# Step 0's scores and exponentials move into the planned projections, and the plan's order changes

## The chip, the cores and the metric

The kernel runs on one core of a Trainium2 chip. The metric is the device time of one execution in microseconds; the time before is the median of three runs, 881.73 us (881.26 to 881.87). The profile is of one execution of its own, which took 882.3 us; its span from the first to the last instruction is 880.5 us, and the 1.8 us between lie outside the instructions.

## The reference

Two mixers read the same input x (2048 x 448, 16 heads of 28) and their outputs are blended by a gate. A looks at 8 positions with a stride of 2, B at all positions. The softmax of B is the bulk of the work.

```python
# A: W, dil = 8, 2
logits = jnp.einsum("bhsd,bhswd->bhsw", q, kg) * scale
logits = jnp.where(mask[None, None, :, :], logits, -1e9)
o = jnp.einsum("bhsw,bhswd->bhsd", _softmax(logits, axis=-1), vg)
# B
scores = jnp.einsum("bhqd,bhkd->bhqk", q, k) * (Dh ** -0.5)
o = jnp.einsum("bhqk,bhkd->bhqd", _softmax(scores, axis=-1), v)
...
g = _sigmoid((x * gate_w).sum(-1, keepdims=True))
return g * a + (1 - g) * b
```

## The kernel before

Everything is scheduled by hand: the order in which the program records instructions is the order in which each engine takes them. Each float32 operand of a product is split into a high and a low part, so a projection and a score are three products each (high x high, low x high, high x low).

**Projections.** 92 output tiles (`tiles`): 28 tiles of B's q and k (128 x 512), 16 of B's v and 48 of A's q, k and v (128 x 448). The first eleven (`FULL`) use the whole array. The next 80, tiles 11 to 90, come from a plan: `quarters()` deals each tile's 42 products to four quarters of 32 rows of the array, which run at the same time, and gives each tile one of the eight PSUM banks `PS[0]` to `PS[7]` (named r0 to r7). A tile's products that belong to different quarters come one quarter after the other. When a tile's last product is sent, ScalarE copies the bank (`qk_tile` or `copy_tile`; an A tile goes to a staging tile `ast` whose store is issued by SP's queue in `a_tile`).

**Maxima.** The softmax of B needs a maximum of a row of scores before the exponentials. Only the high parts are used for that: a maximum is one product of 30 rows in one quarter (`s1_mm`, line 152) and one VectorE reduction over 512 columns (`s1_quarter`, line 174, in the plan; `s1_max`, line 158, in the main loop). There are 1024 in 16 units of 64; 320 are sent in the plan (`MAXIMA`), 80 a quarter. The planner keeps clocks for PE's quarters, VectorE and ScalarE and the time at which each bank comes free. It sends a maximum when VectorE's queue, by its own clocks, is shorter than `HUNGER` (0.1 us) and a bank is free, and no quarter is more than one maximum ahead of another beyond `AHEAD`. q's high part for the next unit is loaded by `load_qhi` (line 104, into `QP`) when a unit is begun or done.

**Main loop.** 256 steps: unit u (four heads, 512 queries) and kt (128 keys). A step takes twelve products of scores (four heads by three, line 1212, `scores`), up to three maxima, two exponentials of two heads each by ScalarE (128 x 1024, line 1217) into pairs `P`, five of which rotate, and the four products with V of the step before (`do_av`, line 1178) into the bank `av`. PSUM is laid out anew for it: three tiles of two banks (T0, T1 and T2, which `ring` turns), the single bank `T1` (line 734) and `av`. A new tile of PSUM may be written only when every reader of the old ones in its banks has finished; `T1` and `av` come from one pool. VectorE's small work, GpSimd's work for mixer A and the loads are hung on the steps (`at`, `issue`, `item`). The last 20 steps are sent by `tail_steps` in an order of their own, with single exponentials of 128 x 512 (line 1355) among them, and the output projection ends the kernel.

**Between the two.** Step 0 is sent after the plan. As it has no step before it whose product with V could stand between its scores and those of step 1, the last projection tile (`last_tile`, line 603, eleven products of the whole array into `av`) stands there.

Of the kernel before, what the change touches and what calls it, by code (L numbers as in the profile page):

```python
# [26 lines left out]
def gated_mix_kernel(ctx: ExitStack, tc: tile.TileContext, xT, xn, gw, wA, wB, woAB, out):  # L27
# [129 lines left out]
    def s1_max(n, k, bank):  # L157
# [5 lines left out]
            finished.append(n // 64)  # L163
        s1c[0] = n + k


    count = [0] * 4

# [64 lines left out]
    if True:  # L233
# [192 lines left out]
        def quarters(n0, n1, maxima):  # L426
            todo = [[n for k in range(n0, n1, 5) for n in (k + i for i in TURN[q]) if n < n1] for q in range(4)]
            cols = {n: 512 if tiles[n][1] == "qk" else D for n in range(n0, n1)}
            left = {n: sum(len(quarter_order(n, q)) for q in range(4)) for n in cols}
            free, ready, sent, stay, home = [0.0] * 8, {}, [0] * 4, [[] for _ in range(4)], {}  # L430
            free[(n0 - 1) % 4] = 2.0
            end, begun = [0.0] * 4, [-1.0] * 4
            now_ = dve = act = issue = 0.0
            plan, round_ = [], []
            while any(todo) or any(stay):
                b = min(range(8), key=lambda i: free[i])

                def start(q, wait):
                    return max(max(issue, wait, begun[q]) + LOAD, end[q], now_)

                best = None
                for q in range(4):
                    wait = 0.0
                    if not stay[q]:
                        n = todo[q][0] if todo[q] else None
                        wait = ready.get(n, free[b]) if n is not None else 1e9
                    p = start(q, wait), 1, q, wait
                    m = start(q, free[b]), 0, q, free[b]
                    if sent[q] < min(maxima // 4, min(sent) + AHEAD + 1) and free[b] < 1e8:
                        lag = dve - m[0] - REACH  # L450
                        if (lag < HUNGER and free[b] <= max(issue, end[q] - LOAD) + 0.02) or (
                                p[0] < 1e8 and p[0] > m[0] + 0.18 and lag < HUNGER + 1.2):
                            p = m
                    if p[0] < 1e8 and (best is None or p < best):
                        best = p
                t, product_, q, wait = best
                if round_ and max(act, round_[0][0]) <= t:
                    act = max(act, round_[0][0]) + 0.64
                    plan.append((t, "round", round_.pop(0)[1]))
                issue, now_, begun[q] = max(issue, wait) + 0.003, t, t  # L460
                if not product_:
                    sent[q] += 1
                    end[q] = t + 0.2315
                    dve = max(dve, t + REACH) + SUM
                    free[b] = dve + 0.092 + WORD
                    plan.append((t, "max", q, b))
                    continue
                if not stay[q]:
                    n = todo[q].pop(0)
                    stay[q] = [(n, p) for p in quarter_order(n, q)]  # L470
                    first = n not in home
                    if first:
                        home[n] = b
                        free[b] = 1e9
                    ready[n] = 1e9
                else:
                    first = False
                n, p = stay[q].pop(0)
                end[q] = t + (0.2315 if cols[n] == 512 else 0.2045)
                left[n] -= 1  # L480
                last, leaves = not left[n], not stay[q]
                plan.append((t, "product", n, p, q, home[n], first, last, leaves and not last))
                if leaves:
                    ready[n] = t + REACH + NOP
                if last:
                    act = max(act, t + REACH)
                    free[home[n]] = act + (0.68 if cols[n] == 512 else 0.62) + WORD
                    act += 0.607 if cols[n] == 512 else 0.553
                    if cols[n] == 512:
                        round_.append((act + 0.1, n))  # L490
            return plan + [(now_, "round", n) for _, n in round_]


# [111 lines left out]
            a_tile(len(tiles) - 1, bank, i, j)  # L605


        FULL, MAXIMA = 11, 320

        parts = []  # L610

# [83 lines left out]
            behind(n)  # L695
        n = FULL
        before(n)
        plan = quarters(FULL, len(tiles) - 1, MAXIMA)
        turns.extend(x[0] + REACH for x in plan if x[1] == "product" and x[8])
        for t, kind, *x in plan:  # L700
            run_jobs(t)
            if kind == "max":
                s1_quarter(x[0], PS[x[1]])
                continue
            if kind == "round":
                qk_round(x[0])
                continue
# [481 lines left out]
    def scores(u, kt, cur):  # L1189
# [9 lines left out]
        for tok in WITH if k else ALONE:  # L1199
            if tok[0] == "s":  # L1200
                i = int(tok[1])
                if i < k:
                    s1_mm(n + i, bank[tok])
                if i == 0:
                    s1_max(n, 1, T1)
                elif i == 2 and k > 1:
                    s1_max(n + 1, k - 1, other[:, 0:k - 1, :])
                continue
            a, t = tok[0], int(tok[1])
            h = (int(a) + n) % 4  # L1210
            r = slice(32 * h, 32 * h + ROWS)
            nc.tensor.matmul(bank[a], (KH[g % 3], KH[g % 3], KL[g % 2])[t][r, ks], (qh, ql, qh)[t][r, :], start=(t == 0), stop=(t == 2))  # L1212
            if t == 2 and a in "20":
                if len(exps) < 5:
                    probs.append(pair("P"))
                p = probs[len(exps) % 5]
                e = nc.scalar.activation(p, one if a == "2" else mine, AF.Exp, scale=SCALE).ins  # L1217
                for o in exps[-5:-4]:
                    tc.declare_no_dep(e, o, query=mybir.DependencyQuery.ANY_SYNC,
                                      reason="PE has read what it wrote, and this one waits for PE")  # L1220
# [66 lines left out]
    def bank_of(m, b):  # L1287
        return m.tiles[b[0]][:, b[1], :] if b[0] else T1

    lastp = {}  # L1290

    def tail_steps(sts, m, waiting, begin, middle, finish):

        left = {}
# [4 lines left out]
        for tok in PERIOD:  # L1299
# [49 lines left out]
            else:  # L1349
# [4 lines left out]
                parts = [(id(p), c)]  # L1354
                e = nc.scalar.activation(p[:, c, :], bank, AF.Exp, scale=SCALE).ins
                m.read[banks[0]] = [*m.read.get(banks[0], ()), e][-3:]
            for part in parts:
                for o in lastp.get(part, ()):
                    tc.declare_no_dep(e, o, query=mybir.DependencyQuery.ANY_SYNC,
                                      reason="PE has read what it wrote, and this one waits for PE")  # L1360
                lastp[part] = [*lastp.get(part, ()), e][-3:]
# [8 lines left out]
    turn = [0]  # L1370

    def pair_p():
        p = probs[turn[0] % 5]
        turn[0] += 1
        return p

    def step_begin(u, kt, st):
        now[0] = st
# [20 lines left out]
    for u in range(NU):  # L1399
        g, b = divmod(u, NB)  # L1400
        for kt in range(NJ):
# [30 lines left out]

    assert s1c[0] == s1e and not finished
    m = Banks()
    turn[0] = len(exps) % 5
    for i, e in enumerate(exps[-5:]):
        p = probs[(len(exps) - 5 + i) % 5 if len(exps) >= 5 else i]
        lastp[id(p), 0], lastp[id(p), 1] = [e], [e]
    waiting = [(NJ * NU - TAIL - 1, prev, 0.5)]

    def tail_finish(st):
# [49 lines left out]
```

## Time and profile before

| | before |
|---|---|
| median of three runs | 881.73 us |
| profiled execution | 882.3 us, span 880.5 us |
| PE / VectorE / ScalarE / GpSimd busy | 99% / 85% / 69% / 62% of the span |
| granted TensorE clock | 1.000 |
| first to last product of the plan's quarters | 34.7 to 236.6 us |
| last tile's first matmul | 238.3 us |
| step 1's first score | 240.8 us |
| first of the 20 last steps | about 768 us |

A row of the timeline gives the start in us, the length, the engine, the line and the operation with its tiles, and how many instructions are merged in it; in brackets the idle time of the engine ahead of it and what ended it. Records of PE overlap, since its matmuls are pipelined and four quarters run at once. A row of a group gives count, busy time, mean length of one in ns, and the idle time ahead. A row of windows gives the stretch, the busy time and, behind x, how many instructions touch it.

### The profile page before, as it was taken

What the parts mean: (1) busy time and instruction counts of PE and PEld (TensorE: products, weight loads), DVE (VectorE), ACT (ScalarE), POOL (GpSimd) and SP (SyncE); (2) the same over time, 40 slices, a digit from 0 to 9 for tenths busy, and PEclk for the clock granted to TensorE, in tenths of its full rate; (3) what the DMA queues carried; (4) which work ended last, traced back from release to release, by engine and by line L of the source; (5) the groups of instructions that cost most, each with busy time, mean ns of one, the idle gap of its engine ahead of it and who ended that gap; (6) DMA issues with size and microseconds to landing.
All of it is one profiled execution on the core that took longest, in us unless ns stands there. A gap on an engine that the chain in (4) does not pass through costs nothing.

```text
span 880.5 us, 24214 instructions
## 1 busy us (share of the span) xinstructions
PE 874.7 (99%) x9988; PEld 522.6 (59%) x9988; DVE 747.7 (85%) x1128; ACT 609.2 (69%) x800; POOL 548.9 (62%) x439
## 2 busy tenths in 40 slices
PE   9999999999999999999999999999999999999998
PEld 6899999999844444444444344444444444434997
DVE  7699999999889999999999999999999999832220
ACT  6353323212388899898888988989989898898120
POOL 1157402110089789998899989999999799701000
PEclk9999999999999999999999999999999999999999
DMA  8858605545564232224235242442131222337781
GB/s 262 266 184 257 201 14 146 121 112 134 116 224 133 74 90 55 89 56 136 73 73 153 63 122 58 109 122 67 47 74 30 83 45 50 105 93 203 197 268 53
DMA packets 114199, 104.76 MB, mean 119 GB/s; under 512 B 75256, under 2 KB 82424, under 8 KB 113304
## 3 DMA queue, kind: packets, MB, share of 16 engines
q1 hardware_dynamic: 113656, 102.42, 41.2%
q8 instruction: 78, 1.28, 0.6%
q10 hardware_dynamic: 432, 0.79, 0.3%
q14 instruction: 33, 0.27, 0.1%
HBM read 62.20 MB, written 40.96 MB: 117 GB/s over the span
## 4 chain that ended last, share of the span: by engine, by line
PE 97%; DVE 1%; ACT 1%; DMA 0%; issue 0%; ACTq 0%
PE T L1212 29%; PE av L1178 29%; PE r L390 14%; PE r L385 8%; PE T L1046 8%; PE T L152 4%; PE r L152 3%; PE T L1329 2%; DVE MX L174 1%; DMA raw<-in_wB 0%; ACT P L1217 0%; PE av L603 0%; ACT ast L526 0%; ACT onhi L1103 0%; ACT wh L576 0%
## 5 line engine op out<-in xcount | busy, mean ns | idle before, releaser
L1217 ACT ACTIVATE P<-T 128x1024 f32<-128x1024 f32 x472 | 458.2, 1024 | 57.5 <-PE T L1212 55.8
L158 DVE TENSOR_REDUCE MX<-T 128x1 f32<-128x512 f32 x470 | 442.2, 953 | 32.2 <-PE T L152 17.9
L1178 PE MATMUL av<-P,V 128*32 128x512 f32 x2048 | 272.7, 605 | 0.0
L152 PE MATMUL T<-KH,QP 30*128 30x512 f32 x704 | 220.9, 458 | 0.0
L1212 PEld LDWEIGHTS T<-QH,KH 30*128 30x128 f32 x944 | 86.8, 181 | 212.6 <-ACT P L1217 196.5
L1212 PE MATMUL T<-QH,KH 30*128 30x512 f32 x944 | 199.9, 488 | 0.5 <-ACT ast L526 0.3
L174 DVE TENSOR_REDUCE MX<-r 128x1 f32<-128x512 f32 x320 | 197.8, 683 | 1.6 <-PE r L152 0.8
L1212 PE MATMUL T<-QH,KL 30*128 30x512 f32 x944 | 176.0, 394 | 0.0
L1212 PE MATMUL T<-QL,KH 30*128 30x512 f32 x944 | 173.7, 389 | 0.0
L390 PE MATMUL r<-wh,xh 32*128 32x448 f32 (+1 forms) x1008 | 152.1, 366 | 0.0
L390 PE MATMUL r<-wl,xh 32*128 32x448 f32 (+1 forms) x882 | 146.8, 362 | 0.0
L390 PE MATMUL r<-wh,xl 32*128 32x448 f32 (+1 forms) x756 | 140.2, 362 | 0.0
L813 POOL TENSOR_TENSOR prod<-qt,kt 128x896 f32<-128x896 f32 x64 | 135.4, 2116 | 3.9 <-DMA kt<-a_scr 3.9
L390 PEld LDWEIGHTS r<-wh,xh 32*128 32x128 f32 x1008 | 130.1, 184 | 1.4 <-ACT zt L538 0.5
L152 PE MATMUL r<-KH,QP 30*128 30x512 f32 x320 | 123.4, 400 | 0.0
L390 PEld LDWEIGHTS r<-wl,xh 32*128 32x128 f32 x882 | 121.2, 184 | 0.1
L390 PEld LDWEIGHTS r<-wh,xl 32*128 32x128 f32 x756 | 111.2, 184 | 0.1
L874 POOL TENSOR_TENSOR oat<-oat,prod 128x896 f32<-128x896 f32 x48 | 101.4, 2112 | 2.0
L152 PEld LDWEIGHTS T<-KH,QP 30*128 30x128 f32 x704 | 86.0, 181 | 25.9 <-ACT P L1217 14.9
L869 POOL TENSOR_TENSOR prod<-vt,L 128x896 f32<-128x896 f32 x56 | 95.5, 1705 | 0.3
L1212 PEld LDWEIGHTS T<-QL,KH 30*128 30x128 f32 x944 | 88.7, 184 | 0.0
L1212 PEld LDWEIGHTS T<-QH,KL 30*128 30x128 f32 x944 | 87.3, 182 | 0.1
(144 smaller groups left out, 1170.4 us busy)
## 6 DMA issues: line engine op xcount, KB each, us to landing
a_scr<-ast SPq DMA_DIRECT2D x24, 448.0 KB
qk_hi<-qkh SPq DMA_DIRECT2D x22, 256.0 KB
rbc<-rs SPq DMA_DIRECT2D x64, 64.0 KB
QP<-qk_hi SPq DMA_DIRECT2D x64, 56.0 KB
KL<-qk_lo SPq DMA_DIRECT2D x16, 224.0 KB
QH<-qk_hi SPq DMA_DIRECT2D x64, 56.0 KB
QL<-qk_lo SPq DMA_DIRECT2D x64, 56.0 KB
qt<-a_scr SPq DMA_DIRECT2D x8, 448.0 KB
```

Of the source, the lines that this page charges most:

```text
L152: nc.tensor.matmul(bank, qhis[u][h % 2][r, 128 * qs:128 * qs + 128], KH[u // NB % 3][r, 512 * kc:512 * kc + 512], start=True, stop=True)
L158: i = nc.vector.tensor_reduce(MX[:, n % NMX:n % NMX + k], bank, axis=X, op=ALU.max)
L174: nc.vector.tensor_reduce(MX[:, n % NMX:n % NMX + 1], bank, axis=X, op=ALU.max)
L385: i = nc.tensor.matmul(bank, ws[c][rows, k, t[4]:t[4] + 128], x, start=first, stop=last)
L390: i = nc.tensor.matmul(bank[:, 0:cols], x, ws[c][rows, k, 0:cols], start=first, stop=last)
L813: nc.gpsimd.tensor_tensor(out=p, in0=qt[c], in1=kvt["k", c % 2][:, HALO - DIL * w:HALO - DIL * w + NJ, :], op=ALU.mult)
L869: nc.gpsimd.tensor_tensor(out=dst.rearrange("p j (h d) -> p j h d", d=DH), in0=kvt["v", c % 2][:, HALO - DIL * w:HALO - DIL * w + NJ, :].r ...
L874: nc.gpsimd.tensor_tensor(out=ows[c % 2][:, :, 0:56] if w == W - 1 else oat[c], in0=oat[c], in1=oat[c, w], op=ALU.add)
L1046: writes(bank, nc.tensor.matmul(bank[:, cols], src, wo[c][k][:, cols], start=(first and k == ks[0] and i == 0), stop=(last and k == ks[-1] ...
L1178: nc.tensor.matmul(av[32 * h:32 * h + 32, :], V[:, kt, 4 * g + h, :], tiles_[h], start=(kt == 0), stop=(kt == NJ - 1), skip_group_check=True)
L1212: nc.tensor.matmul(bank[a], (KH[g % 3], KH[g % 3], KL[g % 2])[t][r, ks], (qh, ql, qh)[t][r, :], start=(t == 0), stop=(t == 2))
L1217: e = nc.scalar.activation(p, one if a == "2" else mine, AF.Exp, scale=SCALE).ins
```

## The change

Four things change.

1. Each quarter of the plan gets one item more at its end: the three score products of one head of step 0 (`score`). Its bank is the one that comes free first among seven; when a head's third product is sent, ScalarE takes the exponential of that one bank (128 x 512) into half a pair `P`. The main loop's step 0 then sends neither scores nor maxima, takes `first` as its exponentials, and goes on to `last_tile`.
2. The bank that is left first (other than the one of the tile before the plan) trades its number with bank 7, which `av` occupies, and `av` has a pool of its own, so that the last tile waits for that bank alone.
3. `MAXIMA` is 324 in place of 320, and `HUNGER` is a table of 26 values, one for each 8 us of the plan, in place of one value.
4. What tells the scheduler that a wait is implied already (`probability`), and the turn of the five pairs (`pair_p`), are written once for all three places that take exponentials.

```diff
+    def score(t, h, bank):
+        qh, ql = Qs[0]
+        r = slice(32 * h, 32 * h + ROWS)
+        nc.tensor.matmul(bank, (KH[0], KH[0], KL[0])[t][r, 0:128], (qh, ql, qh)[t][r, :], start=(t == 0), stop=(t == 2))
+        if t == 2:
+            if not len(first) % 2:
+                pair_p()
+            p, c = probs[len(first) // 2], len(first) % 2
+            first[h] = p[:, c, :]
+            probability([(id(p), c)], nc.scalar.activation(first[h], bank, AF.Exp, scale=SCALE).ins)
...
-        HUNGER, AHEAD = 0.1, 1
+        AHEAD, STRETCH = 1, 8.0
...
-            todo = [[n for k in range(n0, n1, 5) for n in (k + i for i in TURN[q]) if n < n1] for q in range(4)]
+            todo = [[n for k in range(n0, n1, 5) for n in (k + i for i in TURN[q]) if n < n1] + [n1 + q] for q in range(4)]
...
+                s = min(range(7), key=lambda i: free[i])
...
-                        if (lag < HUNGER and free[b] <= max(issue, end[q] - LOAD) + 0.02) or (
-                                p[0] < 1e8 and p[0] > m[0] + 0.18 and lag < HUNGER + 1.2):
+                        h = hunger[min(int(m[0] / STRETCH), len(hunger) - 1)]
+                        if (lag < h and free[b] <= max(issue, end[q] - LOAD) + 0.02) or (
+                                p[0] < 1e8 and p[0] > m[0] + 0.18 and lag < h + 1.2):
...
+                if n >= n1:
+                    plan.append((t, "score", p, q, home[n]))
+                    if last:
+                        act = max(act, t + REACH) + 0.494
+                        free[home[n]] = act + 0.1 + WORD
+                    continue
...
+            b = min((i for i in range(8) if i != (n0 - 1) % 4), key=lambda i: free[i])
+            swap = {b: 7, 7: b}
...
-        FULL, MAXIMA = 11, 320
+        FULL, MAXIMA = 11, 324
...
+        HUNGER = (0.26, 0.3, 0.14, 0.1, 0.1, 0.26, 0.1, 0.03, 0.26, 0, 0, 0.1, 0.18, 0.26, 0.1, 0.1, 0.1, 0.26, 0.26, 0.18, 0.03, 0.3, 0.35, 0.18, 0.1, 0.26)
...
     T1 = pool.tile([128, 512], F32, name="T1")
+    pool = ctx.enter_context(tc.tile_pool(name="psw", bufs=1, space=bass.MemoryType.PSUM))
     av = pool.tile([128, 512], F32, name="av")
...
-            for a in scores(u, kt, cur):
-                if a == 2:
-                    run("mid", st)
+            if st:
+                for a in scores(u, kt, cur):
+                    if a == 2:
+                        run("mid", st)
+            else:
+                cur, left = first, 0
+                run("mid", st)
```

**PE around the last tile.** These are PE's rows of before from the plan's last product (line 390) to the last tile (line 603); r0 to r7 are the plan's banks, T0 to T2 and T1 those of the main loop, QH and QL0 the high and low part of q, KH0 and KL0 those of k, and line 152 is a maximum.

```order
L390 MATMUL r2_136<-wh6_3643,xl1_208 128x448 x3
L1212 MATMUL T2_5199<-QH_4396,KH0_167 128x512 x2
L152 MATMUL T1_5203<-KH1_168,QP10_175 128x512
L1212 MATMUL T2_5199<-QL0_171,KH0_167 128x512 x2
L1212 MATMUL T1_5195<-QH_4396,KH0_167 128x512 x2
L1212 MATMUL T2_5199<-QH_4396,KL0_169 128x512 x2
L1212 MATMUL T1_5195<-QL0_171,KH0_167 128x512 x2
L152 MATMUL T0_5191<-KH1_168,QP11_176 128x512
L152 MATMUL T0_5191<-KH1_168,QP10_175 128x512
L1212 MATMUL T1_5195<-QH_4396,KL0_169 128x512 x2
L603 MATMUL av_5204<-wh6_3643,xh3_206 128x448 x4
```

After the change PE's last rows ahead of the last tile (now line 648) are these; line 187 is a score product of step 0, line 418 a product of the plan.

```order
L187 MATMUL r0_128<-QL0_171,KH0_167 128x512
L187 MATMUL r3_140<-QH_4399,KH0_167 128x512
L418 MATMUL r1_132<-wh6_3644,xl1_208 128x448
L187 MATMUL r0_128<-QH_4399,KL0_169 128x512
L187 MATMUL r3_140<-QL0_171,KH0_167 128x512
L418 MATMUL r1_132<-wh6_3644,xl1_208 128x448
L187 MATMUL r3_140<-QH_4399,KL0_169 128x512
L187 MATMUL r2_136<-QH_4399,KH0_167 128x512
L152 MATMUL r5_148<-KH1_168,QP10_175 128x512
L187 MATMUL r2_136<-QL0_171,KH0_167 128x512
L187 MATMUL r2_136<-QH_4399,KL0_169 128x512
L648 MATMUL av_5238<-wh6_3644,xh3_206 128x448 x4
```

The scores of step 0 moved from the main loop's banks into the plan's, the plan's last products stand among them, and the last tile follows the last score product. The last product into r7, whose bank `av` takes, stands 18 matmuls ahead of the last tile.

**ScalarE at the same place.** Its rows of before, from the copies of the plan's last tiles on (P are the exponentials, nmt and nmv the negated maxima of a unit):

```order
L526 ACTIVATE ast_5169<-r6_152 128x8x56
L526 ACTIVATE ast_5172<-r5_148 128x8x56
L526 ACTIVATE ast_5172<-r2_136 128x8x56
L1217 ACTIVATE P_5219<-T2_5199 128x1024
L1217 ACTIVATE P_5228<-T1_5195 128x1024
L195 ACTIVATE nmt_5232<-m_5230 128x16
L196 ACTIVATE nmv_5233<-m_5230 128x16
L526 ACTIVATE ast_5169<-av_5204 128x8x56
```

And after the change (line 193 is an exponential of one head, 571 a copy, 223 and 224 the negated maxima):

```order
L193 ACTIVATE P_5171<-r2_136 128x512
L571 ACTIVATE ast_5177<-r7_156 128x8x56
L571 ACTIVATE ast_5190<-r4_144 128x8x56
L193 ACTIVATE P_5171<-r0_128 128x512
L571 ACTIVATE ast_5177<-r1_132 128x8x56
L193 ACTIVATE P_5203<-r3_140 128x512
L193 ACTIVATE P_5203<-r2_136 128x512
L223 ACTIVATE nmt_5241<-m_5239 128x16
L224 ACTIVATE nmv_5242<-m_5239 128x16
L571 ACTIVATE ast_5190<-av_5238 128x8x56
```

Two exponentials of 1024 columns became four of 512, and they stand among the copies; the copy of r7 has one exponential right ahead of it. On SP's queue the four loads of q for unit 6 (`QP`), which stood behind the last but one staging tile's store, now stand ahead of it.

More of the change, by code (lines that the diff above doesn't have):

```diff
@@ L164, in s1_max, with pair_p, probability @@
         s1c[0] = n + k
+    turn = [0]
+    lastp = {}
+    first = {}
+    def pair_p():
+        if len(probs) < 5:
+            probs.append(pair("P"))
+        turn[0] += 1
+        return probs[(turn[0] - 1) % 5]
+    def probability(parts, e):
+        for part in parts:
+            for o in lastp.get(part, ()):
+                tc.declare_no_dep(e, o, query=mybir.DependencyQuery.ANY_SYNC,
+                                  reason="PE has read what it wrote, and this one waits for PE")
+            lastp[part] = [*lastp.get(part, ()), e][-3:]
+    def score(t, h, bank):
[8 more added lines that the diff above has]
+            probability([(id(p), c)], nc.scalar.activation(first[h], bank, AF.Exp, scale=SCALE).ins)
     count = [0] * 4
@@ L445, in quarters @@
                         n = todo[q][0] if todo[q] else None
-                        wait = ready.get(n, free[b]) if n is not None else 1e9
+                        wait = 1e9 if n is None else free[s] if n >= n1 else ready.get(n, free[b])
                     p = start(q, wait), 1, q, wait
@@ L490, in quarters @@
                         round_.append((act + 0.1, n))
+            if sum(sent) < maxima:
+                return None
+            b = min((i for i in range(8) if i != (n0 - 1) % 4), key=lambda i: free[i])
+            swap = {b: 7, 7: b}
+            where = {"max": 3, "score": 4, "product": 5}
+            plan = [(*x[:where[x[1]]], swap.get(x[where[x[1]]], x[where[x[1]]]), *x[where[x[1]] + 1:])
+                    if x[1] in where else x for x in plan]
             return plan + [(now_, "round", n) for _, n in round_]
@@ L1213, in scores @@
             if t == 2 and a in "20":
-                if len(exps) < 5:
-                    probs.append(pair("P"))
-                p = probs[len(exps) % 5]
+                p = pair_p()
                 e = nc.scalar.activation(p, one if a == "2" else mine, AF.Exp, scale=SCALE).ins
-                for o in exps[-5:-4]:
-                    tc.declare_no_dep(e, o, query=mybir.DependencyQuery.ANY_SYNC,
-                                      reason="PE has read what it wrote, and this one waits for PE")
+                probability([(id(p), 0), (id(p), 1)], e)
                 for o in maxs[-4:]:
@@ L1356, in tail_steps @@
                 m.read[banks[0]] = [*m.read.get(banks[0], ()), e][-3:]
[L1357 to L1361, printed above, removed]
+            probability(parts, e)
             ready[i] = m.exponential(banks, max(done[i, x] for x in group))
```

29 lines of the change are left out of this document (12 added, 17 removed).

## The prediction

> **What bounds the kernel now.** I read the page first: the span, the engines' shares and the chain that ended last.
>
> ```profile
> span 880.5 us, 24214 instructions
> ...
> PE 874.7 (99%) x9988; PEld 522.6 (59%) x9988; DVE 747.7 (85%) x1128; ACT 609.2 (69%) x800; POOL 548.9 (62%) x439
> ...
> PE 97%; DVE 1%; ACT 1%; DMA 0%; issue 0%; ACTq 0%
> ```
>
> The chain runs through PE for 97% of the span, so work or idle time that leaves PE leaves the time. PE is busy in all but 5.8 us (880.5 less 874.7). But in the projections four quarter matmuls run side by side, and busy time only says that at least one of them ran. So the next view is the windows of PE over the part of the plan that is made of 448-column tiles, twelve stretches of 12 us; the number behind x counts the matmuls in each.
>
> ```profile
> core 0: us, PE busy (x), PEclk, DMA share, GB/s
> 88.00:100.00 12.00, 12.00 (x234) 1.00 0.71 196
> 100.00:112.00 12.00, 12.00 (x238) 1.00 0.52 172
> 112.00:124.00 12.00, 12.00 (x237) 1.00 0.08 22
> 124.00:136.00 12.00, 12.00 (x227) 1.00 0.02 5
> 136.00:148.00 12.00, 12.00 (x230) 1.00 0.69 195
> 148.00:160.00 12.00, 12.00 (x229) 1.00 0.60 135
> 160.00:172.00 12.00, 12.00 (x228) 1.00 0.47 126
> 172.00:184.00 12.00, 12.00 (x236) 1.00 0.42 110
> 184.00:196.00 12.00, 12.00 (x232) 1.00 0.53 123
> 196.00:208.00 12.00, 12.00 (x229) 1.00 0.63 165
> 208.00:220.00 12.00, 12.00 (x239) 1.00 0.32 86
> 220.00:232.00 12.00, 12.00 (x241) 1.00 0.35 80
> ```
>
> Busy reads 12.00 everywhere and the granted clock 1.00, yet the count goes from 227 to 241, with a mean of 2800 / 12 = 233.3. The windows below 241 hold idle quarters, all told 12 x 241 - 2800 = 92 matmuls. At 12 / 233.3 = 0.0514 us a matmul that is 4.7 us in these 144 us, invisible in the busy share. This is what a new order of the plan can win or lose.
>
> [...]
>
> The other engine that works through the whole plan is VectorE, which takes one maximum from each product of scores. Its timeline in pieces, the window sum of those reductions, and their group:
>
> ```profile
> 135.39 21.09 DVE L174 TENSOR_REDUCE MX<-r 128x1 f32<-128x512 f32 x34
> ...
> 180.93 4.86 DVE L174 TENSOR_REDUCE MX<-r 128x1 f32<-128x512 f32 x8
> ```
> ```profile
> 184.00:236.40 52.40, 51.74 (x84) 1.00 0.43 107
> ```
> ```profile
> L174 DVE TENSOR_REDUCE MX<-r 128x1 f32<-128x512 f32 x320 | 197.8, 683 | 1.6 <-PE r L152 0.8
> ```
>
> It looks full: 197.8 us busy and 1.6 us idle. But a reduction's 0.68 us overlaps the next one. Eight in a row take 4.86 us, so they start (4.86 - 0.68) / 7 = 0.597 us apart; the run of 34 has (21.09 - 0.68) / 33 = 0.618. The total of busy and idle, 199.4 us over 320, makes 0.623. So it can go at 0.597 and mostly goes a little slower, because the next product is late. At 0.597, 320 of them are 191.0 us, which leaves some 8 us of slack, less the few small reductions and transposes between them.
>
> **The end of the plan and step 0.** Here is what the change takes out, in PE's timeline:
>
> ```profile
> 235.65 0.36 PE L390 MATMUL r<-wl,xh 32*128 32x448 f32 x1
> 235.85 0.76 PE L390 MATMUL r<-wh,xl 32*128 32x448 f32 x3
> 236.95 0.50 PE L1212 MATMUL T<-QH,KH 30*128 30x512 f32 x2 [0.35 <-ACT ast L526]
> ...
> 237.73 0.39 PE L1212 MATMUL T<-QL,KH 30*128 30x512 f32 x2
> ...
> 237.96 0.40 PE L1212 MATMUL T<-QH,KL 30*128 30x512 f32 x2
> ```
> ```profile
> 238.28 1.09 PE L603 MATMUL av<-wh,xh 128*128 128x448 f32 x4
> ...
> 240.75 0.18 PEld L1212 LDWEIGHTS T<-QH,KH 30*128 30x128 f32 x2 [0.30 <-issue]
> 240.75 0.50 PE L1212 MATMUL T<-QH,KH 30*128 30x512 f32 x2
> ```
>
> The plan's last products end at 235.85 + 0.76 = 236.61. PE then waits 0.35 us for ScalarE's copy of the last tile, runs step 0's twelve score products and three maxima, and begins the last tile at 238.28, or 0.08 us before the last score product ends (237.96 + 0.40 = 238.36).
>
> **Removed: 1.75 us.** If the last tile follows the plan in the same manner, it begins 0.08 us before the plan's last end and not 1.67 us after it (238.28 - 236.61).
>
> **The handoff's new wait: +0.1 us.** The last tile goes into bank 7, and ahead of it stands the copy of the tile that left that bank. In the order, 18 matmuls of PE stand between that tile's last product and the last tile: 18 x 0.0514 = 0.93 us, and 0.3 us more until the last quarter is through. On ScalarE one exponential may stand ahead of the copy. The rows for its queue:
>
> ```profile
> 235.92 1.42 ACT L526 ACTIVATE ast<-r 128x448 f32<-128x448 f32 x3 [0.26 <-PE r L390]
> ```
> ```profile
> L1217 ACT ACTIVATE P<-T 128x1024 f32<-128x1024 f32 x472 | 458.2, 1024 | 57.5 <-PE T L1212 55.8 <-ACT ast L526 0.7
> L526 ACT ACTIVATE ast<-r 128x448 f32<-128x448 f32 x47 | 24.0, 546 | 53.6 <-PE r L390 47.4 <-issue 5.1 <-PE r L152 0.8
> L1355 ACT ACTIVATE P<-T 128x512 f32<-128x512 f32 x40 | 21.8, 599 | 0.1
> ```
>
> Product 0.36, exponential 0.599 at worst, copy 0.546: 1.5 us against 1.23 us. So the wait lies between 0 (ScalarE free) and 0.6 us (one more exponential ahead); I take 0.1, near the lower end, because the exponential's scores end earlier than the product. Two exponentials of 1024 columns become four of 512: 4 x 0.599 against 2 x 1.024, or 0.35 us more on ScalarE. From the bank's copy on, its queue holds three copies, 0.44 us apart by the run of three ((1.42 - 0.546) / 2), and three exponentials of at most 0.599: 3.1 us. The last tile covers 2.47 us (238.28 to 240.75), and the copy begins 1.23 - 0.96 = 0.3 us before the last tile could, so the last exponential ends some 2.8 us behind that start. The pair of banks that it frees is wanted once the next step has sent the six products of its first pair, so at about that moment. I cost this at nothing; without the cover it would be the 0.6 us again.
>
> **Added: +0.92 us.** Twelve score products and one maximum more for each quarter are 16 matmuls, four a quarter. In the same quarters, 237.73 and 237.96 are successive products of 512 columns, 0.23 us apart. 4 x 0.23 = 0.92.
>
> **Of this, idle quarters at the end take 0.4 us.** The three last products (x3, from 235.85) stand in one quarter, the third starts about 0.4 us after the first, while the other three are idle. From about 235.95 to 236.45 that is 3 x 0.5 = 1.5 quarter-us, or 0.4 us of PE, and the scores now stand among the last tile's products. Bounds: 0 and 0.6.
>
> **The new order: -1.0 us.** The order tells that 26 thresholds now decide how eagerly maxima are sent, one for each 8 us; what they save can't be read from it. Bounds from the windows: all at the richest, 241, saves 4.7 us; all at the poorest, 227, costs (233.3 - 227) x 12 x 0.0514 = 3.9 us. A choice by stretch mends poor stretches first. Raising the four poorest (227, 228, 229, 229) to the mean wins 20.3 matmuls, 1.0 us. I take that value, nearer to nothing than to either bound.
>
> **Main loop: -0.1 us.** Of the four maxima that leave it, three were step 0's, counted above; the fourth leaves the last step that has any. That is one quarter's 0.23 us among others: between 0 and 0.23. Everything else keeps its place behind the last tile. Four loads move on SP's queue:
>
> ```profile
> 237.81 2.97 SPq L104 DMA_DIRECT2D QP<-qk_hi  x4
> ...
> 241.43 0.38 SPq L542 DMA_DIRECT2D a_scr<-ast  x1
> ```
>
> They took 2.97 us in step 0; now they stand in the plan, ahead of the store of the last but one staging tile and well before the last tile's store. They wait for the last maximum of the unit whose tile they overwrite, and behind them only stores wait, which nobody needs before the mixer's loads. No cost.
>
> **Sum:** -1.75 + 0.1 + 0.92 - 0.4 - 1.0 - 0.1 = -2.23 us. The profiled execution took 882.3 us (its span is 880.5), so it would take 880.1. The median shown, 881.73, is 0.57 lower: **879.5 us**.
>
> **Rivals.**
> *The order wins nothing.* The scores find no idle quarters and the stretches stay as they are: -1.75 + 0.1 + 0.92 - 0.1 = -0.83, or 880.9. For it: the windows of 208 to 232 are already at 239 and 241. Against it: eight of twelve are below 237.
>
> *VectorE sets the pace.* If the slack of 8 us is not to be had, four more maxima cost 4 x 0.618 = 2.47 us in place of all that the lanes would do: -1.75 + 0.1 + 2.47 - 0.1 = +0.72, or 882.4, slower. It decides from the pace at which 324 maxima take longer than before plus 0.92: (199.4 + 0.92) / 324 = 0.618 us each. For it: the window 184 to 236.4 is 51.74 of 52.40 busy, and the long run already goes at 0.618. Against it: the run of eight at 0.597. [...]
>
> *The order is poorer.* PE takes its queue in order, so one product that waits for a bank holds all four quarters. With all windows at 227, 3.9 us come on top of -0.83: +3.1, or 884.8.
>
> *The order is far better:* all windows at 241, -0.83 - 4.7 = -5.5, or 876.2.
>
> *It doesn't do what it says:* the last tile waits for its bank or the first step for its pair; that is the 0.6 us in the range.
>
> **How the numbers follow.** Forecast 0.66, nothing won 0.16, VectorE 0.11, poorer 0.05, far better 0.02. The range leaves out the last three, 0.18. Its upper end takes the handoff at 0.6 and no gain from tail, order or last step: -1.75 + 0.6 + 0.92 = -0.23, or 881.5. Its lower end takes the handoff at 0, the tail at 0.6, the order at twice its value and 0.23 for the last step: -3.66, or 878.1. Within 0.2% (1.76 us, about what a measurement of this kernel can tell from no change) are a tenth of the forecast, the case without gain and the VectorE case but for its tail: 0.32. Faster 0.63, slower 0.05.
>
> **What would show it.** Right: the last tile's first matmul at about 236, before 238.28; the score products end within 0.1 us of it; PE's windows of 12 us average 236 or more; the reductions' mean distance falls to about 0.615. Wrong: a wait of PE for ScalarE ahead of the last tile (handoff), a first step that begins over 2.6 us behind the last tile's start (cover), window counts at 233 (nothing won), or reductions without pauses at 0.618 and more (VectorE). If the last tile is early but the end isn't, the main loop gave it back.

## The result, and the profile after

The changed kernel took 888.02 us in the median of six runs (885.57 to 890.35) against 881.8 (881.26 to 882.94): a ratio of 1.007, 95% interval 1.0053 to 1.0088. It is slower by 6 us, where 2.2 us less was forecast, and lies far outside the range. Its runs also scatter over 4.8 us, those of before over 1.7.

The profiled execution is the slowest of the six, 890.35 us. Its page:

```profile
span 888.6 us, 24220 instructions
...
PE 878.8 (99%) x9988; PEld 523.3 (59%) x9988; DVE 747.0 (84%) x1129; ACT 608.3 (68%) x802; POOL 549.1 (62%) x440
...
PEclk9998999999999999999999999999999999999999
...
PE 96%; SPq 1%; DVE 1%; DMA 1%; issue 1%; ACT 0%; POOL 0%; POOLq 0%; ACTq 0%
```

Two things are new: the granted clock has a digit 8 in the fourth slice, and the chain leaves PE for SP's queue, a DMA and "issue". Windows of PE around that slice (busy time, matmuls behind x, then the clock):

```profile
60.00:80.20 20.20, 20.20 (x347) 1.00 0.78 219
80.20:85.10 4.90, 0.21 (x4) 0.91 0.78 235
85.10:91.90 6.80, 6.77 (x76) 0.56 0.77 248
91.90:104.00 12.10, 12.10 (x231) 1.00 0.64 197
```

PE stands for 4.7 us at 80 us, and in the 6.8 us behind that it gets 0.56 of the clock and sends 76 matmuls, where the rate of the first row gives 117. 41 matmuls at 20.2 / 347 = 0.058 us are another 2.4 us. The chain at that place tells who held it (PE's own pieces left out):

```profile
80.27 0.73 POOL qkr L308
81.00 0.30 SPq L104
81.31 0.04 issue
81.35 0.60 SPq L104
81.95 0.04 issue
81.99 2.94 DMA qk_hi<-qkr
...
85.03 0.05 ACT qkh L555
```

Read from the end: ScalarE's rounding of a q or k tile (`qkh`, line 555) waits for a store out of the buffer that it is to write. That store lands 2.94 us after 81.99. It is issued so late because SP's queue takes its stores in order, and those ahead wait for GpSimd's low parts (`qkr`, line 308; the last ends at 81.00). SP's timeline shows what else was ahead:

```profile
74.72 2.97 SPq L104 DMA_DIRECT2D QP<-qk_hi  x4
78.69 1.23 SPq L104 DMA_DIRECT2D qk_hi<-qkh  x2
80.01 1.93 SPq L104 DMA_DIRECT2D qk_lo<-qkr  x2
81.99 0.59 SPq L104 DMA_DIRECT2D qk_hi<-qkr  x1
```

And the waits of 76 to 92 us say why PE stands with ScalarE:

```profile
ACT qkh L555 <- DMA qk_hi<-qkr: 6.0, 1, 6.0
POOL qkr L308 <- ACT qkh L555: 5.8, 1, 5.8
...
PE r L418 <- ACTq L426: 4.7, 1, 4.7
```

Line 426 is the word that hands a tile's bank from one quarter to the next: an empty instruction of ScalarE or GpSimd. Here it stood in ScalarE's queue behind the rounding, and PE, in order, held all four quarters for it: four matmuls touch those 4.9 us. The loads `QP` are those of unit 2. They are issued when unit 1's maxima may begin, and the new order has 64 maxima done earlier: the loads now stand ahead of the stores of the five tiles that end at that time, not among them. In SP's timeline of the kernel before, the store out of `qkr` goes out ahead of the loads, at 78.77:

```profile
78.77 0.33 SPq L104 DMA_DIRECT2D qk_hi<-qkr  x1
...
81.68 2.19 SPq L104 DMA_DIRECT2D QP<-qk_hi  x4
84.02 0.34 SPq L104 DMA_DIRECT2D qk_hi<-qkh  x1
```

The order of things at the end of the plan is as forecast, in PE's timeline:

```profile
244.98 0.39 PE L187 MATMUL r<-QH,KL 30*128 30x512 f32 x1
245.29 1.08 PE L648 MATMUL av<-wh,xh 128*128 128x448 f32 x4
...
247.73 0.50 PE L1264 MATMUL T<-QH,KH 30*128 30x512 f32 x2
```

The last score product ends at 245.37, the last tile begins 0.08 us before that, and step 1 follows 2.44 us later. But all of it is 7.0 us later than before: from the plan's first product to the last tile it took 211.35 us (33.94 to 245.29), before 203.60 (34.68 to 238.28). From the first to the last product with V the main loop took 568.6 us, before 567.6: the other 1.0.

### The profile page after: what moved, and what is told of

Same layout as the page of the kernel before. It is cut to its first block, busy times and chain, and to the rows that moved or that the text cites. A ratio compares the mean times of both kernels' runs of the same rounds, so it can differ in the third digit from the quotient of the medians.

```text
span 888.6 us, 24220 instructions
## 1 busy us (share of the span) xinstructions
PE 878.8 (99%) x9988; PEld 523.3 (59%) x9988; DVE 747.0 (84%) x1129; ACT 608.3 (68%) x802; POOL 549.1 (62%) x440
## 4 chain that ended last, share of the span: by engine, by line
PE 96%; SPq 1%; DVE 1%; DMA 1%; issue 1%; ACT 0%; POOL 0%; POOLq 0%; ACTq 0%
PE av L1230 28%; PE T L1264 28%; PE r L418 15%; PE r L413 8%; PE T L1098 8%; PE T L152 4%; PE r L152 3%; PE T L1375 2%; DVE MX L158 1%; PE r L255 1%; SPq L104 0%; DMA fsum<-rs 0%; DMA qk_hi<-qkr 0%; SPq L938 0%; PE av L648 0%
## 5 line engine op out<-in xcount | busy, mean ns | idle before, releaser
L202 DVE TENSOR_REDUCE MX<-r 128x1 f32<-128x512 f32 x324 | 200.1, 682 | 9.5 <-PE r L152 7.7
L418 PE MATMUL r<-wh,xh 32*128 32x448 f32 (+1 forms) x1008 | 154.1, 368 | 5.4 <-ACTq L426 4.7
L418 PE MATMUL r<-wl,xh 32*128 32x448 f32 (+1 forms) x882 | 149.2, 366 | 0.0
L418 PE MATMUL r<-wh,xl 32*128 32x448 f32 (+1 forms) x756 | 143.6, 365 | 0.0
L418 PEld LDWEIGHTS r<-wl,xh 32*128 32x128 f32 x882 | 124.1, 185 | 0.0
L418 PEld LDWEIGHTS r<-wh,xl 32*128 32x128 f32 x756 | 114.7, 186 | 0.1
```

The costliest lines, as they stand in the source:

```text
L202: nc.vector.tensor_reduce(MX[:, n % NMX:n % NMX + 1], bank, axis=X, op=ALU.max)
L418: i = nc.tensor.matmul(bank[:, 0:cols], x, ws[c][rows, k, 0:cols], start=first, stop=last)
```

## The experiments

Each was run against the kernel before on the same chip; runs 1 to 4, 5 to 8 and 9 to 12 had a chip each, on which the kernel before took 881.88, 881.97 and 881.85 us. Times within a run are those of its one profiled execution. "Loop" is the time from the first to the last step's product with V in the profile; before it is 567.6.

**1. The loads of unit 2 later.**

```diff
-                if done < MAXIMA:
+                if done == 64:
+                    soon(12.0, lambda: load_qhi(2))
+                elif done < MAXIMA:
                     load_qhi(done // 64 + 1)
```

> The changed kernel, but the four loads of q for unit 2 (QP) are issued 12 us of the plan later, behind the stores of the five tiles that end there. Theory Q (SP's queue: the loads, which the new order puts ahead of those stores, hold them up, ScalarE waits for a store, and PE's next product for ScalarE): the 4.7 us stop of PE at 80 us and the half clock behind it are gone, and the time is 879 to 881 us. Rival R (the new order sends the five tiles' work too tightly for the ring of eight pairs, wherever the loads stand): the stop stays, 885 to 890 us.

Measured 886.27 us, ratio 1.0053 (1.0041 to 1.0065). The stop shrank from 4.7 to 3.3 us, with 3.4 us of half clock behind it (the mean clock of this execution is 0.998). Theory Q missed, and the time lies where rival R has it: most of the stop stays without the loads. The 1.4 us between the two stops are a difference of single executions and no firm price of the loads; the profile of run 3, with the loads in the early place, has a stop of 2.6.

**2. The move alone,** with one threshold and 320 maxima; the three maxima that step 0 sent follow the last tile.

```diff
-        FULL, MAXIMA = 11, 324
+        FULL, MAXIMA = 11, 320
...
-        HUNGER = (0.26, 0.3, 0.14, 0.1, 0.1, 0.26, 0.1, 0.03, 0.26, 0, 0, 0.1, 0.18, 0.26, 0.1, 0.1, 0.1, 0.26, 0.26, 0.18, 0.03, 0.3, 0.35, 0.18, 0.1, 0.26)
+        HUNGER = (0.1,)
...
                 last_tile(av)
+                n = s1c[0]
+                one, mine, other = ring
+                ring[:] = (one, other, mine)
+                for i, bank in enumerate((T1, other[:, 0, :], other[:, 1, :])):
+                    s1_mm(n + i, bank)
+                s1_max(n, 1, T1)
+                s1_max(n + 1, 2, other[:, 0:2, :])
```

> The move alone: step 0's scores and exponentials in the plan, but one threshold (0.1) and 320 maxima as before; three maxima that stood in step 0 are sent right behind the last tile. The loads of q for unit 2 stand behind the stores, as before. By the terms of the prediction: -1.75 + 0.1 + 3 x 0.23 - 0.4 for the move and +0.35 for three maxima behind the last tile, -1.0 us: 880.8. Theory Q expects no stop of PE at 80 us. If the move were what hurts (rival M: a bank or exponential at the end of the plan is late), it is slower than before, 883 or more.

Measured 884.18 us, ratio 1.0023 (1.0012 to 1.0033), 3.4 more than expected. No stop at 80 us, and the last tile begins at 236.78, 1.5 us earlier than before, of which 0.6 is an earlier start of the plan (34.07 against 34.68). But its own extra maxima made PE wait for VectorE's reductions (0.5 and 0.6 us idle at 240 and 241 us), the clock halved for 3.4 us behind that (mean 0.998), and the loop took 569.3. The move's first half is right; the run can't tell what it is worth.

**3. The order alone:** the new thresholds, with 320 maxima; the quarters end without the scores, and step 0 takes scores, exponentials and maxima itself, as before.

```diff
-            todo = [[n for k in range(n0, n1, 5) for n in (k + i for i in TURN[q]) if n < n1] + [n1 + q] for q in range(4)]
+            todo = [[n for k in range(n0, n1, 5) for n in (k + i for i in TURN[q]) if n < n1] for q in range(4)]
...
-        FULL, MAXIMA = 11, 324
+        FULL, MAXIMA = 11, 320
...
-            if st:
+            if True:
```

> The order alone: the new table of thresholds with 320 maxima, but step 0 sends its scores and maxima after the plan as before. The loads of q for unit 2 stand ahead of the stores, as in the changed kernel. Theory Q and rival R: PE stops at 80 us, the clock halves behind it, 885 to 890 us. Rival M: no stop, 880 to 882 us.

Measured 888.78 us, ratio 1.0078 (1.0065 to 1.0091): as slow as the whole change. The stop is there (2.6 us idle in the profile), and the loop is 567.7, as before. So the order makes the stop without the move. The five runs show the clock's part: 885.75 us at a mean clock of 1.000, 887.46 at 0.998, and 888.78 to 889.65 at 0.996.

**4. The loads' place, put into the kernel before.**

```diff
+            if done == 60:
+                for i in range(4):
+                    dma_r(QL[1][32 * i:32 * i + DH, :], qk_hi[DH * i:DH * i + DH, 0:512])
...
-                if done < MAXIMA:
+                if done == 64:
+                    soon(12.0, lambda: load_qhi(2))
+                elif done < MAXIMA:
```

> The kernel before, with nothing of the change but the suspected cause: four loads of the same size, into a spare tile, are issued at the place of SP's queue where the changed kernel has those of q for unit 2, and the real ones 12 us of the plan later. Theory Q: ScalarE waits for a store and PE for ScalarE, 2 to 5 us, and the clock may halve: 884 to 890 us. Rival R: as before, 881.5 to 883 us.

Measured 882.86 us, ratio 1.0012 (1.0003 to 1.002). PE now waits 0.9 us, up to 85.25, for a word behind ScalarE. The time lies in rival R's range and under theory Q's, though the kernel is about 1 us slower and the wait is the one that theory Q names: the loads' place is a part of the cause and can't make the stop alone.

**5. The move alone, without extra maxima behind the last tile.** 320 maxima and one threshold as in 2; the three stay for the steps from 1 on, and the last unit's negated maxima are loaded two steps later, so that they are stored first.

```diff
-        elif u + 2 == NU and kt == 12:
+        elif u + 2 == NU and kt == 14:
             load_nm(u + 1)
```

> The move alone without the three maxima behind the last tile, whose waits spoiled the run before: scores and exponentials of step 0 in the plan, one threshold 0.1, 320 maxima, all others from step 1 on (the last two in step 235), and the load of the last unit's negated maxima two steps later. Theory Q (the new order does the harm, the move does what was forecast): the last tile begins at 236.8 us as in the run before, step 1 right behind it, 1.5 us earlier than in the kernel before, and step 235 pays 0.3 for its two maxima: 880.3 to 881 us. Rival M (the move itself costs elsewhere): 882 or more.

Measured 882.27 us, ratio 1.0013 (1.0002 to 1.0024): missed, and in rival M's range. The last tile is again at 236.77, 1.5 us earlier; 1.0 of that is a shorter plan (202.56 us from its first product, before 203.60), the rest an earlier start. The loop is 569.0, 1.4 longer, and takes all of it back: 0.6 at three steps of 2.55 us and around them, 0.1 in step 235, and 0.6 in the steps to 240, where this run's own later load is used. The prediction's "everything else keeps its place" was the doubtful sentence. Eight of the eleven runs lie between 881.87 and 882.41 us, but three took 885.1 to 887.0, two of these at mean clocks of 0.998 and 0.996. The profile is of one of the eight, so what made the three longer was not seen, and the move alone is not cleared of it.

**6. High parts stored at once** in the changed kernel: `qk_store` gets an argument that names which of the two parts (0 high, 1 low) it stores, so that the high part's store no longer waits for GpSimd's low part.

```diff
-            low_part(lo, raw, hi, 0.75, lambda: soon(0.9, lambda: qk_store(nb, rows, hi, lo)))
+            soon(1.2, lambda: qk_store(nb, rows, hi, lo, (0,)))
+            low_part(lo, raw, hi, 0.75, lambda: soon(0.9, lambda: qk_store(nb, rows, hi, lo, (1,))))
```

> The changed kernel, but each q and k tile's high part is stored as soon as ScalarE has rounded it, and only the low part's store waits for GpSimd. Theory S (the store that ScalarE waits for stands on SP's queue behind stores that wait for GpSimd's low parts): the stop of PE at 80 us falls from 4.7 us to under 2.5, time 882 to 886 us. Rival R (the ring of pairs is too short, whatever the stores' order): the stop stays at 3 us or more, 885 to 890 us.

Measured 882.85 us, ratio 1.0009 (1.0000 to 1.0018): 5 us less than the changed kernel by one store's place in a queue. ScalarE's timeline at the place:

```profile
79.46 0.63 ACT L555 ACTIVATE qkh<-qkr 128x512 fp32r<-128x512 f32 x1
80.43 0.63 ACT L555 ACTIVATE qkh<-qkr 128x512 fp32r<-128x512 f32 x1 [0.34 <-PE r L418]
82.98 1.15 ACT L555 ACTIVATE qkh<-qkr 128x512 fp32r<-128x512 f32 x2 [1.91 <-DMA qk_hi<-qkh]
```

The wait of 6.0 us is 1.9, the longest pause between two of PE's matmuls there is 0.4, and the clock is whole (mean 1.000). Theory S holds.

**7. Spare tiles** in the changed kernel: ScalarE needs no buffer of the ring for the tiles 21 to 25.

```diff
+        SPARE = {21: 15, 22: 7, 23: 14, 24: 6, 25: 13}
...
-            hi, raw = ptile("qkh").bitcast(F32R), raws_.pop(n)
+            raw = raws_.pop(n)
+            hi = (V[:, SPARE[n], :, :].rearrange("p h e -> p (h e)") if n in SPARE else ptile("qkh")).bitcast(F32R)
```

> The changed kernel, but the five high parts of the tiles 21 to 25 are written into memory of V that is idle at that time, in place of halves from the ring of pairs, so that ScalarE has no store to wait for there. Theory B (ScalarE, waiting for a buffer of the ring, holds the word that hands a bank from one quarter to the next, and PE with it): the stop of 4.7 us at 80 us is gone, the clock stays whole, 881 to 883 us; the smaller stops at 125, 167 and 206 us and the slower main loop remain, so it isn't faster than before. Rival (PE stops for another reason at that place): 885 to 890 us.

Measured 885.84 us, ratio 1.0049 (1.0033 to 1.0064): the time missed, for a reason of its own. The stop at 80 us is gone, but a new one of 3.4 us stands at 98: GpSimd fills V with ones there, waits 5.0 us in all for the stores out of V, and a word (L426) that PE needs stands behind it in GpSimd's queue. It is the same mechanism on the other engine.

**8. The same, and GpSimd's low part of the negated maxima later.**

```diff
-                parts.append((n + 3, u, max_parts(u)))
+                parts.append((n + 3, u, max_parts(u, lambda f: soon(1.2, f))))
```

> As the run with spare tiles, and GpSimd's low part of a unit's negated maxima is issued 1.2 us of the plan later, so that GpSimd doesn't stand still for VectorE and ScalarE with a handing-over word behind. Theory H (the stops at 125, 167 and 206 us, together 1.6 us, are words that wait behind that instruction): 1.0 to 1.6 us less than the run with spare tiles, 880 to 881.5 us. Rival: the same as that run within 0.3 us.

Measured 885.1 us, ratio 1.0035 (1.0023 to 1.0047), 0.7 less than run 7 where 1.0 to 1.6 was expected. The runs of the two scatter over 5.2 and 2.4 us, so their times can't decide; the absolute time is off for the reason named there. In the profiles the last tile goes from 242.65 to 240.57 us: 0.45 of that is the stop at 98, 0.15 an earlier start of the plan, and the other 1.5 us are the three smaller stops, which are gone. Run 10 tests this without the large stop. What they were shows in the chain of the changed kernel:

```profile
122.88 0.53 POOL KL L87
123.41 1.55 issue
124.96 0.03 POOLq L426
124.99 0.04 issue
125.03 0.47 PE r L418
```

At this unit's end GpSimd's instruction waits 1.59 us for ScalarE's, and ScalarE's 1.75 us for VectorE's; a word behind it (L426) waits along, and PE with it (0.4 us for the word). At 206 us the word again stands behind 1.54 us of "issue".

**9. The steps aligned.** High parts at once as in 6, and step 1 sends two maxima, so that after it as many are sent as in the kernel before.

```diff
-                cur, left = first, 0
+                cur, left = first, 3
...
-        k = min(3, s1e - n)
+        k = min(2 if n == MAXIMA else 3, s1e - n)
```

> The changed kernel with the high parts stored at once, and step 1 sends two maxima in place of three, so that from then on every unit of maxima ends in the same step as in the kernel before. Theory A (the main loop lost 1 to 1.9 us because the units end a step earlier, which slides mixer A's stores on SP's queue ahead of a sum's load, and rounding on ScalarE onto the exponentials): the loop from the first to the last product with V goes back from 569.4 to 567.7 +- 0.2 us and the long steps 71 and 126 are gone; 880.8 to 881.5 us. Rival (the loop is slower for another reason, as the banks that the plan leaves): the loop stays at 568.6 to 569.5 us, the time at 882.5 to 883.

Measured 881.71 us, ratio 0.9999 (0.999 to 1.0007), 0.2 above the expected range and 1.1 less than run 6. The loop goes from 569.4 to 567.8, and the long steps are gone. One of them, step 71, in SP's timeline of the changed kernel:

```profile
392.70 0.52 SPq L1122 DMA_DIRECT2D rs<-osb  x1
393.31 3.04 SPq L938 DMA_DIRECT2D oa_scr<-tw  x4
...
398.37 2.90 SPq L938 DMA_DIRECT2D oa_scr<-tw  x4
...
404.98 1.93 SPq L1126 DMA_DIRECT2D fsum<-rs  x1
```

and in that of the kernel before:

```profile
380.47 3.03 SPq L886 DMA_DIRECT2D oa_scr<-tw  x4
...
385.45 3.11 SPq L886 DMA_DIRECT2D oa_scr<-tw  x4
388.66 0.54 SPq L1070 DMA_DIRECT2D rs<-osb  x1
...
394.62 0.37 SPq L1074 DMA_DIRECT2D fsum<-rs  x1
```

With 324 maxima and a step 0 that sends none, units end a step earlier. That moves VectorE's small work, mixer A's eight stores (`oa_scr`) slide from ahead of a sum's store to behind it, and the sum's load (`fsum`) is issued 12.3 us after its store (before 6.0). VectorE waits for that load with a reciprocal at the head of its queue:

```profile
408.32 0.25 DVE L1130 RECIPROCAL finv<-fsum 128x16 f32<-128x16 f32 x1 [0.67 <-DMA fsum<-rs]
```

**10. All three:** as 9, with the later low part of 8.

> As the run before with the units aligned, and GpSimd's low part of a unit's negated maxima 1.2 us of the plan later. By theory H the three smaller stops of the plan, 1.6 us together, go; by theory A the loop is 567.7 us. The last tile then begins at 236.7 us, the span is 879.1 and the time 880.4 to 881 us: faster than before by 1.0 to 1.5 us, about half of what was forecast for the change.

Measured 880.01 us (879.41 to 880.61, eleven runs), ratio 0.9979 (0.997 to 0.9988), 0.4 below the expected range and faster than both kernels. Against run 9, from which it differs by the later low part alone, it is 1.7 us faster in the medians, and the plan up to the last tile is 1.6 us shorter (201.68 against 203.30): theory H's 1.6 us. The page's chain, and PE at the end of the plan:

```profile
PE 98%; ACT 1%; DMA 0%; issue 0%; DVE 0%; ACTq 0%
...
L202 DVE TENSOR_REDUCE MX<-r 128x1 f32<-128x512 f32 x324 | 198.8, 681 | 1.1 <-PE r L187 0.2
```
```profile
235.18 0.38 PE L187 MATMUL r<-QH,KL 30*128 30x512 f32 x1
235.49 1.08 PE L649 MATMUL av<-wh,xh 128*128 128x448 f32 x4
...
237.93 0.49 PE L1265 MATMUL T<-QH,KH 30*128 30x512 f32 x2
```

The last tile begins 2.8 us earlier than before (238.28), of which 0.9 is an earlier start of the whole plan in this execution (33.81 against 34.68).

**11. The kernel before with the two cures of the plan:** the edits of 6 and 8 (high parts at once, GpSimd's low part of the negated maxima later), in the kernel before.

> The kernel before with the two cures of the plan alone (high parts stored at once, the low part of the negated maxima later), no part of the change. It has no stop of PE over 0.36 us in the plan, so by theories S and H it gains next to nothing: 881.5 to 882.2 us. Rival: the cures are worth something by themselves, then it comes to 880.5 to 881.2, and the gain of the run with all three isn't the change's.

Measured 881.41 us (880.88 to 882.09), ratio 0.9995 (0.9986 to 1.0004): no gain that can be told from none. None of its runs is as fast as the slowest of run 10.

**12. The order alone with the two cures:** the edits of 3, with those of 6 and 8.

> The order alone (new thresholds, 320 maxima, step 0 as before) with the same two cures. By theories S and H the stops (2.6 and 1.6 us) that put its last tile at 241.6 us are gone: it begins at 237.2 to 237.6, against 238.3 before, which is the forecast's 1.0 us for the order; 880.7 to 881.3 us. Rival: the new order wins nothing even without stops: 881.7 to 882.5 us.

Measured 880.70 us (880.29 to 881.26), ratio 0.9986 (0.9977 to 0.9995). The last tile begins at 236.72 us; the stops are gone. Against run 11 the order brings 0.7 us in the medians, and the move with its four maxima and the aligned steps, from here to run 10, another 0.7.

## Why the prediction was wrong

**Right: what is taken out at the end of the plan.** The last tile begins 0.08 us before the last score product ends, as in the term of 1.75 us; the handoff cost nothing (0.1 was taken); the cover of 2.47 us held: step 1 came 2.44 us after the last tile began. From the plan's first product to the last tile, the kernel before took 238.28 - 34.68 = 203.60 us, run 10 235.49 - 33.81 = 201.68: 1.9 us less, where the terms up to the main loop's gave 2.13. Of the 1.9, 0.25 belongs to the cures (run 11 took 203.35). The move's own terms were somewhat too good: -1.13 us, against -0.6 from run 12 to run 10, and -1.36 without the four maxima, against -1.0 in run 5. Which of them is short was not told apart.

**Right in size, once nothing stops it: the order.** 1.0 us was taken from raising the poorest windows. Run 12 took 236.72 - 34.41 = 202.31 us to its last tile, and run 11 237.24 - 33.88 = 203.36: 1.05 us. In the time it is 0.7. The mechanism is the forecast one too: in the prediction's twelve windows run 12 sends 2820 matmuls, run 11 2799 and the kernel before 2800, and the four poorest (227, 228, 229 and 229) hold 238, 233, 237 and 235 in run 12, while the two richest lose 4 each. The sign that was named for being right, an average of 236 or more, was too high for this gain; run 12 has 235.0, run 10 234.8.

**Wrong: "The new order", as a term that can only win or lose idle quarters.** Its bounds were window counts of an execution that had no stop. The trace of before held the danger in plain sight, in ScalarE's waits for stores and loads ahead of that same rounding, and they were not read because no engine waited for ScalarE there:

```profile
82.27 1.15 ACT L510 ACTIVATE qkh<-qkr 128x512 fp32r<-128x512 f32 x2 [1.83 <-DMA qk_hi<-qkh]
84.19 1.15 ACT L510 ACTIVATE qkh<-qkr 128x512 fp32r<-128x512 f32 x2 [0.77 <-DMA QP<-qk_hi]
```

The order moved the place of the loads, of GpSimd's low parts and of the words, and the wait came to stand ahead of a word. The plan up to the last tile became 7.75 us longer. Set product by product against run 10, whose plan sends the same products in the same order, the change loses 5.1 us at the stop, 2.8 from there to 104 us (the half clock and the restart), and 0.9, 0.5 and 0.4 at the ends of three units: 9.7 us, the 7.75 and run 10's gain of 1.9. The rival "the order is poorer" named the right mechanism, one product in order that holds four quarters (4.7 us), but had it wait for a bank, priced it by poor windows at 3.9 us and gave it 0.05.

**Wrong: "Main loop: -0.1" and "everything else keeps its place behind the last tile".** It lost 1.0 us in the profile of the change, 1.4 in run 5, and 1.7 to 2.3 in runs 1, 6 and 7. A step's place in the loop decides when a unit ends, and with it what shares a step on VectorE, ScalarE and SP's queue. Run 9 shows it by putting the units back: 567.8 us for the loop, against 569.4 in run 6.

**Wrong: "They wait for the last maximum of the unit ... No cost",** said of SP's loads of q. It looked at the four loads of unit 6 at the end of the plan alone; the new order had moved those of unit 2 as well, and these have a part in the stop (runs 1 and 4: 1.4 us less without them there, 0.9 us of waiting with them in the kernel before).

**Not the cause: VectorE as the pace.** In the changed kernel its reductions stand idle for 9.5 us in all, 7.7 of them for PE. In run 10 the 324 reductions take 199.9 us with their idle time, 0.617 each, next to the rival's 0.618, and only 1.1 us of it is idle; yet that run is faster, where the rival had +0.72. Whether VectorE could go faster there, and so how near it is to bounding this plan, no run shows.

The sum of the change's profile closes: +7.75 for the plan, +1.05 for the loop and -0.74 for the earlier start of the plan make +8.06, and the span grew by 8.0. Open is which of the new thresholds makes GpSimd's low parts late.

## What to carry to other kernels

When a reordering is priced by busy time, ask of each empty or small instruction that hands something over whose queue it stands in, and what that queue's next waits are; a wait that nobody feels today is a stop as soon as such an instruction comes to stand behind it (ScalarE's 1.83 and 0.77 us in the kernel before cost nothing, its 6.0 us in the change stopped PE for 4.7). Stores that free buffers should not wait behind stores that need another engine's work: in run 6 that place in the queue was worth 5 us. If a loop's work is hung on step numbers, a change that shifts a counter by one against the steps should be realigned or priced as a change of the whole loop (1.6 us between runs 6 and 9).

## What the runs showed of the hardware

A stop of PE can cost more than its length, and not in every run. One kernel, the order alone, took 885.75 us at a whole clock, 887.46 at 0.998 and up to 889.65 at 0.996; only the first of these runs was profiled, and whether the stop was of the same length in the others was not seen. In the profiles the half clock lasts 3.4 us (runs 1, 2 and 7, each with a mean clock of 0.998) or 6.83 us (the change, mean 0.996); run 8's mean clock is 0.997. At half speed 3.4 us lose 1.7, and the second run of the five is 1.7 us behind the first. Of the change's 6.83 us, 0.93 lay in the stop itself, so the loss is under 3 us; the count of matmuls gave 2.4:

```profile
84.20:91.03 6.83, 5.90 (x60) 0.50 0.90 297
```

Half clock followed stops of 4.7 (the change), 3.4 (run 7), 3.3 (run 1) and 2.9 us (run 8), and in run 2 two pauses of 0.55 and 0.63 us close together. These are the windows of the order alone, where no half clock followed 2.6 us of standing still:

```profile
78.00:80.80 2.80, 2.79 (x48) 1.00 0.89 281
80.80:83.40 2.60, 0.00 (x0) 1.00 0.93 316
83.40:90.20 6.80, 6.79 (x124) 1.00 0.85 267
```

So the length of one stop does not tell whether half clock follows. What else decides it, and how long it then lasts, no run shows.
